# Routing of batches 1 and 2 beside another layer, and a last layer whose batch is chosen by numbers on the chip

## The chip, the cores and the metric

One core of a Trainium2 chip runs the whole program. TensorE (PE) does the matmuls, VectorE (DVE), ScalarE (ACT) and GpSimd (POOL) the work on elements, and SyncE (SP) issues most transfers, in the order of its queue. The metric is the device time of one execution in microseconds, as a median over runs. Engines work their instruction streams in order and wait for each other by semaphores. The order of each stream is fixed when the program is built: a scheduler places the instructions that the Python code below issues, and may move them against each other within what the data allow.

## The reference

Three stages, float32. Attention over 4 batches, 8 heads, 576 positions and 64 dimensions, in a linear form with 128 random features; its result, 2304 x 512, goes through two mixture-of-experts layers with 8 experts each.

```python
def phi(x):
    proj = np.einsum('bhsd,df->bhsf', x, w_phi)
    proj = proj - np.max(np.abs(proj), axis=-1, keepdims=True)
    return np.concatenate([np.exp(proj), np.exp(-proj)], axis=-1)
q_p, k_p = (phi(q), phi(k))
...
# first layer: for each expert e
out[mask] = gate_w[mask, None] * (np.maximum(x[mask] @ w1[e], 0.0) @ w2[e])
...
# second layer, capacity 576: token i goes to its best expert e
if counts[e] < capacity:
    disp[e, counts[e]] = x[i]; pos[i] = counts[e]; counts[e] += 1; keep[i] = True
...
h = np.maximum(np.einsum('ecd,edf->ecf', disp, w1), 0.0)
y = np.einsum('ecf,efd->ecd', h, w2)
# kept tokens:
out[i] = gate_w[i] * y[expert_idx[i], pos[i]]
```

Tokens that find their expert full give rows of zeros.

## The kernel before

**Tiles.** Tokens lie in the free dimension, features in the partitions: a batch's input of a layer is a tile `xd` of 128 x 4 x 578 (576 tokens in two halves of 288, and two columns for a common part that is kept apart). In this data all 576 tokens of a batch go to one expert. The kernel takes that as given, checks it on the chip (`bad`), and holds a general version behind a branch that is not taken here. So a layer (w, b), that is MoE layer w on batch b, is two products with the weights of one expert: `layer()` runs eight units `f` of the first product (`ps_h`, L796, evicted by DVE as `hd`, L807), calls `done()`, and then four blocks `d` of the second (`ps_y`, L830). In the second MoE layer DVE multiplies the block by the gate row `gr` (L852) and SP sends it out (L856, L859).

**Weights.** A layer has 16 units of 256 KB. `Stream` fetches them: SP reads the expert index from the chip (`value_load`, L747) when a layer's first unit is due, and then issues transfers into five buffers `wst` (L750). ACT converts a unit to `wh` (L765); DVE, for every third one, or POOL computes the rest `wl` (L767). Five converted units form a ring. Layers that were added to the stream follow each other in it.

**Routing.** `route(b, 2, ...)` is a generator: logits of batch b's 576 tokens, the best expert of each as one-hot rows (128 x 5 x 8), a count per expert, the capacity, the kept tokens' count, and `count()` with the expert's index `exi`, and a flag `act2`: whether any token of the batch is kept. `run_c` carries the counts from batch to batch, so the routings of layer 2 run in the order of the batches. `route1(b)` is the same for layer 1 without capacity, `gate_row(b)` lays the gates out as a row `gr` (L315, L319).

**The order.** `ORDER` is (1,0), (1,1), (2,0), (1,2), (1,3), (2,1). Beside each layer run attention steps, by `RATIO`, and the generators in `side`, up to `SIDE` = 5 steps at each of the layer's yields; `done()` finishes what is left of them before the second half of the layer, and adds the next layer to the stream. Batch 1's routing of layer 2 stands beside (1,3), behind batch 3's of layer 1, batch 2's too; batch 3's stands beside (2,1). Batches 2 and 3 of layer 2 come last, each under a branch on its flag. In this data batch 2 keeps no token, so its output is written as zeros, and batch 3 keeps all of its own. The weights for the first branch that is taken are fetched ahead of the branch, by an index `nxi` that is computed from both flags; inside the branch the ring goes on.

```python
side += {...
         (1, 2): [route1(2)],
         (1, 3): [route1(3), route(1, 2, ps_, "tr"), route(2, 2, ps_, "tr")],
         (2, 1): [route(3, 2, ps_, "tr")]}[which, b]
```

Of the kernel before, what the change touches and what calls it, by code (L numbers as in the profile page):

```python
# [36 lines left out]
SIDE = 5  # L37
# [6 lines left out]
def fused_kernel(ctx: ExitStack, tc: tile.TileContext, kq, v, wphi, emb, tau, w1, wg, w2, cap, out):  # L44
# [96 lines left out]
    def drain(g):  # L141
        for _ in g:
            pass
# [14 lines left out]
    act2 = [slots.tile([1, 1], F32, name=f"act2_{b}") for b in range(B)]  # L158
    act2i = [slots.tile([1, 1], I32, name=f"act2i_{b}") for b in range(B)]
    nxf = slots.tile([1, 1], F32, name="nxf")  # L160
    nxi = slots.tile([1, 1], I32, name="nxi")
# [50 lines left out]
    def route(b, which, ps_pool, ps_tag):  # L212
# [64 lines left out]
        if which == 2:  # L277
            T.matmul(pc[:, 1], tri_b, ohb, start=True, stop=True)
        tot = small.tile([128, 2, NT, E], F32, tag="tot", name="tot")
        V.tensor_copy(tot[:, 0:which], pc[:, 0:which])  # L280
        yield
        if which == 2:
            rk = small.tile([128, NT, E], F32, tag="rk", name="rk")
            for t in range(NT):
                V.tensor_tensor(out=rk[:, t, :], in0=tot[:, 1, t, :], in1=run_c, op=ALU.add)
                V.tensor_tensor(out=run_c, in0=run_c, in1=tot[:, 0, t, :], op=ALU.add)
                if t % 2:
                    yield
            V.tensor_scalar(rk, rk, cap_f, None, op0=ALU.is_lt)
            V.tensor_tensor(out=oh, in0=oh, in1=rk, op=ALU.mult)  # L290
            yield
            kp = small.tile([128, NT], F32, tag="kp", name="kp")
            V.tensor_reduce(out=kp, in_=oh, axis=AX.X, op=ALU.add)
            V.tensor_tensor(out=gt, in0=gt, in1=kp, op=ALU.mult)

            V.tensor_tensor(out=gt, in0=gt, in1=gts[1, b], op=ALU.mult)
            yield
            ohb2 = small.tile([128, NT, E], BF16, tag="ohb", name="ohb2")
            V.tensor_copy(ohb2, oh)
            pk = ps_pool.tile([128, NT, E], F32, tag=ps_tag, name="ps_ck")  # L300
# [910 lines left out]
```

## Time and profile before

| | |
|---|---|
| median of 3 runs | 544.06 us (543.0 to 547.17) |
| profiled execution, its own time | 545.21 us |
| its span | 543.5 us |
| PE busy | 431.3 us, 79% |
| DVE busy | 383.4 us, 71% |
| ACT busy | 242.5 us, 45% |
| POOL busy | 246.8 us, 45% |
| granted TensorE clock, mean | 0.896 |
| transfers | 49.71 MB, 91 GB/s over the span |

The span is what the profiler saw from the first to the last instruction; the profiled execution's own time is 1.7 us longer. Times in the rows are microseconds from the start of the span. An engine is busy while it executes; register, branch and transfer-issuing instructions don't count. "<-" behind a row names the engine and the instruction that ended the idle time ahead of it. The granted clock is given in parts of full speed.

### The profile page before, as it was taken

To read this page: it belongs to the slowest core of one execution; us is meant where nothing else is said; L and a number is where in the kernel's file an instruction comes from. 1 tells how busy PE (TensorE), PEld (TensorE's weight loads), DVE (VectorE), ACT (ScalarE), POOL (GpSimd) and SP (SyncE) were. 2 spreads that over 40 slices of the span, in tenths; PEclk is the share of its full clock that TensorE was granted. 3 is DMA by queue.
4 is the path that set the end of the run, shared out by engine and by line. 5 is a ranking of instruction groups with operands and counts; after the bars stand their busy time and mean duration, and the time that the engine had idled before them with its cause. 6 is when DMAs were issued, how large, how long until landed. Compare 5 with 4: busy or idle time off the path is not lost. (4 is left out here: it accounts for less than half of the span.)

```text
span 543.5 us, 10208 instructions
## 1 busy us (share of the span) xinstructions
PE 431.3 (79%) x3509; PEld 337.7 (62%) x3509; DVE 383.4 (71%) x1213; ACT 242.5 (45%) x539; POOL 246.8 (45%) x255
## 2 busy tenths in 40 slices
PE   5787887893896989779899979894997775792575
PEld 4465664563675876456778667673795663681474
DVE  3876456379989356489857897799555966987383
ACT  4656066162566176371757524462545342320230
POOL 5354445346277135593475533754543321530251
PEclk9979789887997999999899989997998795896678
DMA  6212000044250010633322420731104403512732
GB/s 210 69 48 86 25 26 26 0 136 148 75 198 7 1 26 0 224 127 90 117 58 61 147 77 23 249 118 39 40 2 153 139 20 119 173 43 87 262 118 93
DMA packets 24718, 49.71 MB, mean 91 GB/s; under 512 B 3448, under 2 KB 4536, under 8 KB 24656
## 3 DMA queue, kind: packets, MB, share of 16 engines
q1 hardware_dynamic: 24544, 48.89, 28.2%
q8 instruction: 31, 0.51, 0.4%
q14 instruction: 31, 0.25, 0.2%
q0 software_dynamic: 32, 0.03, 0.0%
q10 hardware_dynamic: 80, 0.03, 0.0%
HBM read 44.22 MB, written 4.72 MB: 90 GB/s over the span
## 5 line engine op out<-in xcount | busy, mean ns | idle before, releaser
L767 POOL TENSOR_TENSOR wl<-wst,wh 128x512 bf16<-128x512 f32 x64 | 82.5, 1297 | 75.8 <-ACT wh L765 71.2
L474 POOL TENSOR_SCALAR qa<-qf 128x1152 f16<-128x1152 f32 x32 | 100.1, 3136 | 30.7 <-ACT qf L472 30.3
L420 PE MATMUL ps_pj<-wb,raw 128*128 128x256 f32 x288 | 88.1, 441 | 30.6 <-DVE s L435 10.7
L765 ACT ACTIVATE wh<-wst 128x512 fp32r<-128x512 f32 x96 | 59.5, 627 | 81.2 <-PE ps_h L796 34.0
L420 PEld LDWEIGHTS ps_pj<-wb,raw 128*128 128x128 f32 x288 | 57.3, 217 | 43.2 <-issue 19.6
L483 PE MATMUL ps_vk<-kf,vr 128*65 128x256 f32 (+1 forms) x320 | 79.5, 387 | 0.8 <-PE ps_r L404 0.8
L830 PE MATMUL ps_y<-hd,wh 128*128 128x290 f32 (+1 forms) x448 | 77.8, 312 | 2.0 <-DVE hd L807 2.0
L796 PE MATMUL ps_h<-xd,wh 128*128 128x290 f32 (+1 forms) x256 | 54.2, 348 | 27.5 <-DVE hd L807 17.1
L425 DVE TENSOR_REDUCE mall<-ps_pj 128x4 f32<-128x512 f32 (+1 forms) x80 | 50.2, 630 | 24.0 <-PE ps_pj L420 23.7
L448 ACT ACTIVATE kf<-s,lnk 128x512 f32<-128x512 f32 (+1 forms) x96 | 57.0, 648 | 19.4 <-DVE s L435 19.4
L830 PEld LDWEIGHTS ps_y<-hd,wh 128*128 128x128 f32 x448 | 63.2, 189 | 3.6 <-ACT wh L765 1.7
L807 DVE TENSOR_SCALAR hd<-ps_h,sc,hd 128x288 fp32r<-128x288 f32 x112 | 59.8, 566 | 5.2 <-PE ps_h L796 4.8
L796 PEld LDWEIGHTS ps_h<-xd,wh 128*128 128x128 f32 x256 | 42.0, 217 | 32.4 <-issue 26.4
L483 PEld LDWEIGHTS ps_vk<-kf,vr 128*65 128x65 f32 (+1 forms) x320 | 39.2, 136 | 32.8 <-issue 16.5
L796 PE MATMUL ps_h<-yd,wh 128*128 128x290 f32 (+1 forms) x192 | 41.9, 365 | 19.4 <-DVEq L973 8.9
L435 DVE TENSOR_TENSOR s<-ps_pj,mall 128x512 f32<-128x512 f32 (+1 forms) x80 | 49.6, 628 | 3.2 <-ACT kf L448 1.5
L796 PEld LDWEIGHTS ps_h<-yd,wh 128*128 128x128 f32 x192 | 34.0, 236 | 22.4 <-ACTq L973 9.0
L767 DVE TENSOR_TENSOR wl<-wst,wh 128x512 bf16<-128x512 f32 x32 | 31.0, 970 | 13.8 <-ACT wh L765 13.6
L472 ACT ACTIVATE qf<-tr 128x512 f32<-128x512 f32 x64 | 33.8, 598 | 6.2 <-PE tr L466 6.0
L531 PE MATMUL ps_nm<-kvh,qa 128*128 128x65 f16 x320 | 32.5, 197 | 0.0
L532 PE MATMUL ps_nm<-kvl,qa 128*128 128x65 f16 x320 | 32.4, 198 | 0.0
L528 PE MATMUL ps_nm<-kcl,ones_h 128*128 128x65 f16 x160 | 30.1, 200 | 0.9 <-POOL kcl L518 0.9
(246 smaller groups left out, 757.5 us busy)
## 6 DMA issues: line engine op xcount, KB each, us to landing
wst<-in_w SPq DMA_DIRECT2D x96, 256.0 KB, 2.9
raw<-in_kq SPq DMA_DIRECT2D x15, 576.0 KB, 5.5
vr<-in_v SPq DMA_DIRECT2D x16, 325.0 KB, 5.5
wfx<-in_w SPq DMA_DIRECT2D x16, 256.0 KB, 2.9
out_t<-o SPq DMA_DIRECT2D x9, 288.0 KB, 2.1
out_t<-zero SPq DMA_DIRECT2D x1, 1152.0 KB, 5.0
out_t<-o SPq DMA_DIRECT2D x6, 144.0 KB, 2.5
raw<-in_kq SPq DMA_DIRECT2D x1, 288.0 KB, 3.8
```

Source lines behind the costliest of these rows:

```text
L420: T.matmul(ps[:, k_], d["raw"][:, sl], wb, start=True, stop=True)
L425: V.tensor_reduce(out=mall_of[b][:, p, U[0]:U[0] + len(U), :], in_=st[i]["pj", u][:, 0:len(U)], axis=AX.X, op=ALU.max, apply_absolute_valu ...
L435: V.tensor_tensor(out=s[:, 0:n], in0=d["pj", u][:, 0:n], in1=m.unsqueeze(3).to_broadcast([128, n, 2, 128]), op=ALU.subtract)
L448: A.activation(out=d["kf"][0:n, t0:t0 + nk, :, sg, :], in_=d["su", u][0:n, 0:nk], func=AF.Exp, bias=lnk[0:n], scale=(1.0 - 2.0 * sg) / SC)
L472: A.activation(out=d["qf"][:, h, sg, 0:512], in_=d["tr", h], func=AF.Exp, scale=(1.0 - 2.0 * sg) / SC)
L474: G.tensor_scalar(d["qa"][:, h, :, 0:S], d["qf"][:, h], -1.0, None, op0=ALU.add)
L483: T.matmul(ps[:, h, :], d["vr"][0:n, t, h, :], d["kf"][0:n, t, h].rearrange("p s f -> p (s f)"), start=(t == 0), stop=(t == NT - 1))
L765: A.activation(out=h, in_=src, func=AF.Copy)
L767: q.tensor_tensor(out=l, in0=src, in1=h.bitcast(F32), op=ALU.subtract)
L796: T.matmul(ps[:, 0:n], wh[:, c, :], x[:, c, hf * HALF:hf * HALF + n], start=(c == 0), stop=(c == 3 and not hf))
L807: V.tensor_scalar(hd[:, f, hf * HALF:(hf + 1) * HALF], ps[:, 0:HALF], sc[:, f:f + 1], nm, op0=ALU.add, op1=ALU.max)
L830: T.matmul(ps[hf][:, 0:w], wh[:, j, :], hd[:, k_, hf * HALF:hf * HALF + w], start=(k_ == 0), stop=(k_ == 7 and not hf))
```

## The change

Routing: `route(1, 2)` and batch 1's gate row move from beside layer (1,3) and the start of (2,1) to beside layer (1,2). `route(2, 2)` comes first beside (1,3), then `route1(3)`, and what is left of them at the layer's middle is no longer finished there. `SIDE` is 3 beside (1,3) and (2,1).

Counting in layer 2: the rank of a token within its expert, which took ten operations of 128 x 8 on DVE, becomes four more small matmuls into one PSUM tile, one addition and one fused compare and multiply; the counts are taken on all 128 partitions, and the copies out of PSUM go.

The last layer: (2,3) stands in `ORDER` behind (2,1), in the same weight stream. `choose()` blends batch 2 and batch 3 by their flags: the input (x = x3 * act3 + x2 * (1 - act3), four ACT and four DVE operations of 128 x 578), the gates, the expert's index and the two output offsets, so that the batch that is active is computed and written to its place, and zeros to the other's. Only when both are active is there a branch, for batch 2, behind it.

```diff
-SIDE = 5
+SIDE = {(1, 3): 3, (2, 1): 3}
...
-        if which == 2:
-            T.matmul(pc[:, 1], tri_b, ohb, start=True, stop=True)
-        tot = small.tile([128, 2, NT, E], F32, tag="tot", name="tot")
-        V.tensor_copy(tot[:, 0:which], pc[:, 0:which])
...
-            for t in range(NT):
-                V.tensor_tensor(out=rk[:, t, :], in0=tot[:, 1, t, :], in1=run_c, op=ALU.add)
-                V.tensor_tensor(out=run_c, in0=run_c, in1=tot[:, 0, t, :], op=ALU.add)
...
+        T.matmul(pc[:, 1], tri_b, ohb, start=True, stop=False)
+        for t in range(NT - 1):
+            n = NT - 1 - t
+            T.matmul(pc[:, 1, t + 1:NT], ones_b, ohb[:, t:t + 1, :].to_broadcast([128, n, E]), start=False,
+                     stop=(n == 1))
...
+        V.tensor_tensor(out=rk, in0=pc[:, 1], in1=run_c.unsqueeze(1).to_broadcast([128, NT, E]), op=ALU.add)
+        V.scalar_tensor_tensor(out=oh, in0=rk, scalar=cap_f, in1=oh, op0=ALU.is_lt, op1=ALU.mult)
...
+        T.matmul(pk, ones_b, ohb2, start=True, stop=True)
+        tot = small.tile([128, E], F32, tag="tot", name="tot")
+        V.tensor_reduce(out=tot, in_=pc[:, 0].rearrange("p t e -> p e t"), axis=AX.X, op=ALU.add)
...
+        V.tensor_tensor(out=run_c, in0=run_c, in1=tot, op=ALU.add)
...
-            ORDER = [(1, 0), (1, 1), (2, 0), (1, 2), (1, 3), (2, 1)]
+            ORDER = [(1, 0), (1, 1), (2, 0), (1, 2), (1, 3), (2, 1), (2, 3)]
...
+            def choose():
+                V.tensor_scalar(two, act2[3], -1.0, 1.0, op0=ALU.mult, op1=ALU.add)
+                f0 = nxf[:, 0:1]
+                V.tensor_tensor(out=f0, in0=exf[2, 3], in1=exf[2, 2], op=ALU.subtract)
+                V.tensor_tensor(out=f0, in0=f0, in1=act2[3][0:1], op=ALU.mult)
+                V.tensor_tensor(out=f0, in0=f0, in1=exf[2, 2], op=ALU.add)
+                V.tensor_scalar(nxi[:, 0:1], f0, -1.0, float(E), op0=ALU.mult, op1=ALU.add)
...
+                for c in range(4):
+                    A.activation(out=x[:, c], in_=x[:, c].bitcast(F32), func=AF.Copy, scale=act2[3])
+                    V.scalar_tensor_tensor(out=x[:, c], in0=y[:, c].bitcast(F32), scalar=two,
+                                           in1=x[:, c].bitcast(F32), op0=ALU.mult, op1=ALU.add)
+                    yield
...
-                    while side:
+                    while side and ORDER[k] != (1, 3):
                         side_step()
...
-                         (1, 2): [route1(2)],
-                         (1, 3): [route1(3), route(1, 2, ps_, "tr"), route(2, 2, ps_, "tr")],
-                         (2, 1): [route(3, 2, ps_, "tr")]}[which, b]
+                         (1, 2): [route(1, 2, ps_, "tr"), route1(2), row(1)],
+                         (1, 3): [route(2, 2, ps_, "tr"), route1(3)],
+                         (2, 1): [route(3, 2, ps_, "tr"), choose()],
+                         (2, 3): [row(3)]}[which, b]
...
+                if (which, b) == (2, 3):
+                    SP.dma_start(out=out[:, bass.ds(SP.value_load(nxi[0:1, 2:3], min_val=2 * S, max_val=3 * S), S)]
+                                 .rearrange("(d p) n -> p d n", p=128),
+                                 in_=zero.unsqueeze(1).to_broadcast([128, 4, S]))
+                    at = SP.value_load(nxi[0:1, 1:2], min_val=2 * S, max_val=3 * S)
...
-            first_units(nxi)
...
-            on = {b: nc.values_load(act2i[b][0:1, 0:1], min_val=0, max_val=1) for b in (2, 3)}
-            for b in (2, 3):
-                with tc.If(on[b] > 0) as br:
-                    ws.restart(w2, exi[2, b], True)
-                    BASE[2, b] = 0
-                    drain(layer(b, 2))
...
+            both = nc.values_load(nxi[0:1, 3:4], min_val=0, max_val=1)
+            with tc.If(both > 0):
...
+                drain(layer(2, 2))
```

**The order on SP around the first weights of layer (2,1).** Before, with `exi2_1_111` as batch 1's index for layer 2:

```order
L750 DMA wst_5662<-in_w1 128x512
L750 ISA
L750 DMA wst_5717<-in_w1 128x512
L747 TENSOR_LOAD exi2_1_111
L747 ISA x2
L750 ISA
L750 DMA wst_5784<-in_w2 128x512
```

After, at the same place (the last transfers of (1,3), the first of (2,1)):

```order
L747 DMA wst_5649<-in_w1 128x512
L747 ISA
L747 DMA wst_5687<-in_w1 128x512
L747 ISA
L747 DMA wst_5740<-in_w2 128x512
```

The read of the index has gone from between the two layers; it now stands a layer earlier, among the transfers of (1,2).

**The order on SP behind the last weights of (2,1).** Before, up to the first weights of the last layer (`wfx`):

```order
L971 TENSOR_LOAD act2i_2_120
L971 ISA x2
L859 DMA out_t<-o_6222 128x576
L859 DMA out_t<-o_6258 128x576
L859 DMA out_t<-o_6294 128x576
L856 DMA out_t<-o_6326 128x288 x2
L971 TENSOR_LOAD act2i_3_121
...
L747 TENSOR_LOAD nxi_123
L747 ISA x2
L750 ISA
L750 DMA wfx_6379<-in_w2 128x512
```

After:

```order
L854 DMA out_t<-o_6345 128x288 x2
L965 TENSOR_LOAD nxi_119
L965 ISA x2
L965 REGISTER_ALU
L965 DMA out_t<-zero_5916 128x4x576
L968 TENSOR_LOAD nxi_119
...
L744 TENSOR_LOAD nxi_119
L744 ISA x2
L747 ISA
L747 DMA wst_6228<-in_w2 128x512
```

The block of zeros, which stood behind the last layer's branch, and the reads of three numbers more now stand between the output of (2,1) and the weights of the last layer.

**The order on DVE from the flag of batch 3 to the last layer.** Before (`nxf`, `nxi` are the index of the chosen expert):

```order
L343 CAST act2i_3_121<-act2_3_117 1x1
...
L954 TENSOR_TENSOR nxf_122<-nxf_122,act2_2_116 1x1
L955 TENSOR_TENSOR nxf_122<-nxf_122,exf2_3_105 1x1
L956 TENSOR_SCALAR nxi_123<-nxf_122 1x1
L315 COPY gr_6425<-ps_g_6426 128x512
L319 COPY gr_6425<-ps_g2_6432 128x64
L767 TENSOR_TENSOR wl0_150<-wfx_6379,wh0_149 128x512
L767 TENSOR_TENSOR wl3_156<-wfx_6382,wh3_155 128x512
L971 TENSOR_LOAD act2i_2_120
L973 COMPARE_AND_BRANCH
L803 TENSOR_SCALAR hd_146<-ps_h_6465 128x1
```

After (`yd_5728` is batch 3's input of layer 2, `yd_5194` batch 2's):

```order
L932 SCALAR_TENSOR_TENSOR gt_6021<-gt_5450,two_120,gt_6021 128x5
L937 SCALAR_TENSOR_TENSOR yd_5728<-yd_5194,two_120,yd_5728 128x578
...
L937 SCALAR_TENSOR_TENSOR yd_5728<-yd_5194,two_120,yd_5728 128x578 x2
L924 TENSOR_TENSOR nxf_118<-nxf_118,exf2_2_104 1x1
L316 COPY gr_6422<-ps_g_6423 128x512
L320 COPY gr_6422<-ps_g2_6429 128x64
L937 SCALAR_TENSOR_TENSOR yd_5728<-yd_5194,two_120,yd_5728 128x578
L925 TENSOR_SCALAR nxi_119<-nxf_118 1x1
L940 CAST xb_5914<-yd_5728 128x8
L764 TENSOR_TENSOR wl1_149<-wst_6228,wh1_148 128x512
```

The four blends and the gate row now stand ahead of the chosen index; the residuals `wl` follow behind it, and no branch.

## Rows read from the trace of the kernel before

**Rows 1.** Stages of the last third: each engine's busy time in a stretch.
```profile
core 0: us, PE busy (x) PEld busy (x) DVE busy (x) ACT busy (x) POOL busy (x), PEclk, DMA share, GB/s
349.30:409.30 60.00, 51.82 (x483) 42.02 (x484) 43.54 (x152) 29.84 (x69) 28.83 (x23) 0.91 0.19 59
409.30:415.30 6.00, 2.91 (x22) 1.49 (x21) 3.05 (x27) 2.39 (x6) 0.00 (x0) 1.00 0.38 107
415.30:445.70 30.40, 26.05 (x206) 23.43 (x207) 24.46 (x88) 12.94 (x25) 13.90 (x11) 0.83 0.37 118
445.70:458.10 12.40, 3.35 (x21) 2.00 (x20) 8.43 (x58) 2.58 (x7) 0.21 (x2) 0.58 0.17 41
458.10:489.50 31.40, 26.61 (x213) 23.83 (x214) 27.04 (x89) 10.52 (x18) 14.20 (x11) 0.90 0.40 129
489.50:509.10 19.60, 3.29 (x15) 2.08 (x14) 10.85 (x61) 3.38 (x6) 2.77 (x3) 0.56 0.42 141
509.10:536.70 27.60, 24.79 (x192) 22.97 (x192) 18.00 (x47) 6.50 (x11) 10.31 (x8) 0.82 0.46 152
536.70:543.50 6.80, 0.03 (x2) 0.00 (x0) 1.10 (x3) 0.00 (x0) 0.00 (x0) 0.72 0.27 94
```

**Rows 2.** Timeline of PE: start, us, instruction, and what ended the idle time before.
```profile
458.11 3.82 PE L796 MATMUL ps_h<-yd,wh 128*128 128x290 f32 x16 [2.88 <-ACT wh L765]
...
509.08 1.30 PE L796 MATMUL ps_h<-yd,wh 128*128 128x290 f32 x4 [8.87 <-DVEq L973]
...
513.83 1.32 PE L796 MATMUL ps_h<-yd,wh 128*128 128x288 f32 x8
...
519.98 1.31 PE L796 MATMUL ps_h<-yd,wh 128*128 128x290 f32 x4 [2.81 <-DVE hd L807]
```

**Rows 3.** Timeline of DVE and SP ahead of layer (2,1).
```profile
453.73 0.13 DVE L340 TENSOR_SCALAR exi<-fm 1x1 int32<-1x1 f32 x1
...
454.69 20.21 SPq L750 DMA_DIRECT2D wst<-in_w  x16
```

**Rows 4.** Timeline of all engines ahead of the last layer.
```profile
496.54 0.20 DVE L303 COPY tot<-ps_ck 128x40 f32<-128x40 f32 x1
...
497.28 0.13 DVE L342 TENSOR_SCALAR act<-fmx 1x1 f32<-1x1 f32 x1
...
499.29 0.14 DVE L956 TENSOR_SCALAR nxi<-nxf 1x1 int32<-1x1 f32 x1
...
500.40 10.06 SPq L750 DMA_DIRECT2D wfx<-in_w  x10
...
503.18 0.63 ACT L765 ACTIVATE wh<-wfx 128x512 fp32r<-128x512 f32 x1 [11.40 <-DMA wfx<-in_w]
...
508.05 0.69 DVE L767 TENSOR_TENSOR wl<-wfx,wh 128x512 bf16<-128x512 f32 x1 [3.51 <-ACT wh L765]
```

**Rows 5.** Single lines from 280 us on: least, median and greatest ns, first and last.
```profile
L852 DVE SCALAR_TENSOR_TENSOR o<-ps_y,ny,gr x24: 495/509/518, 335.5 to 537.4; 128x288 f32<-128x288 f32 x24
L315 DVE COPY gr<-ps_g x4: 671/678/692, 326.1 to 500.0; 128x512 f32<-128x512 f32 x4
L285 DVE TENSOR_TENSOR rk<-tot,run_c x20: 150/166/1279, 318.8 to 495.1; 128x8 f32<-128x8 f32 x20
```

**Rows 6.** Timelines of DVE and POOL at one place beside layer (1,2).
```profile
361.44 3.12 DVE L585 TENSOR_SCALAR hi__4695<-n 128x5 f32<-128x5 f32 x1
...
361.39 3.15 POOL L474 TENSOR_SCALAR qa<-qf 128x1152 f16<-128x1152 f32 x1 [0.25 <-ACT qf L472]
```

**Rows 7.** Page, transfers: count, KB each, us from issue to landing.
```profile
out_t<-zero SPq DMA_DIRECT2D x1, 1152.0 KB, 5.0
```

**Rows 8.** Two stretches of the last layer, columns as in the first group.
```profile
519.90:526.50 6.60, 6.52 (x36) 6.11 (x37) 6.60 (x18) 1.26 (x2) 3.82 (x4) 0.53 0.53 155
526.50:536.70 10.20, 10.20 (x98) 9.56 (x96) 6.44 (x18) 2.53 (x4) 2.93 (x3) 1.00 0.30 111
```

More of the change, by code (lines that the diff above doesn't have):

```diff
@@ L157, in fused_kernel @@
     exi = {(w, b): slots.tile([1, 1], I32, name=f"exi{w}_{b}") for w in (1, 2) for b in range(B)}
[L158 to L161, printed above, removed]
+    act2 = [slots.tile([128, 1], F32, name=f"act2_{b}") for b in range(B)]
+    nxf = slots.tile([1, 4], F32, name="nxf")
+    nxi = slots.tile([1, 4], I32, name="nxi")
+    two = slots.tile([128, 1], F32, name="two")
     def add_bad(cond_ok):
@@ L306, in route @@
-        if which == 1:
-            yield from count(b, which, tot)
+        if which == 1:
+            yield
+            yield from count(b, which, pc[:, 0])
+            return
+        T.matmul(pc[:, 1], tri_b, ohb, start=True, stop=False)
[3 more added lines that the diff above has]
+                     stop=(n == 1))
+        V.tensor_tensor(out=gt, in0=gt, in1=gts[1, b], op=ALU.mult)
@@ L309, in gate_row @@
+        tot = small.tile([128, E], F32, tag="tot", name="tot")
+        V.tensor_reduce(out=tot, in_=pc[:, 0].rearrange("p t e -> p e t"), axis=AX.X, op=ALU.add)
+        yield
+        V.tensor_tensor(out=run_c, in0=run_c, in1=tot, op=ALU.add)
+        kp = small.tile([128, NT], F32, tag="kp", name="kp")
+        V.tensor_reduce(out=kp, in_=oh, axis=AX.X, op=ALU.add)
+        yield
+        V.tensor_tensor(out=gt, in0=gt, in1=kp, op=ALU.mult)
+        yield from count(b, which, pk)
     def gate_row(b, which, gd, ps_pool, ps_tag):
@@ L322, in count @@
     def count(b, which, tot):
-        cnt = small.tile([1, 1, E], F32, tag="cnt", name="cnt")
-        V.tensor_reduce(out=cnt[:, 0, :], in_=tot[0:1, 0].rearrange("p t e -> p e t"), axis=AX.X, op=ALU.add)
+        cnt = small.tile([128, 1, E], F32, tag="cnt", name="cnt")
+        V.tensor_reduce(out=cnt[:, 0, :], in_=tot.rearrange("p t e -> p e t"), axis=AX.X, op=ALU.add)
         yield
-        _, cmx, crev = yield from first_max(cnt, 1, 1, "ct")
+        _, cmx, crev = yield from first_max(cnt, 128, 1, "ct")
+        if which == 2:
+            V.tensor_scalar(act2[b], cmx[:, 0:1], 0.0, None, op0=ALU.is_gt)
+        cnt, cmx, crev = cnt[0:1], cmx[0:1], crev[0:1]
         ok = small.tile([1, 1], F32, tag="ok", name="ok")
@@ L754, in fetch, with ahead @@
                     return True
[L756 removed]
+                def ahead(self, n):
                     while self.nu <= n:
[L759 removed]
+                        while self.nf < self.nu + NST and self.fetch():
                             pass
@@ L781, in sums, with layer @@
                 return ps_.tile([128, HALF + 2], F32, tag=tag, name=name)
-            def layer(b, which, done=None):
+            def layer(b, which, done=None, at=None):
+                at = b * S if at is None else at
                 base = BASE[which, b]
@@ L903, in prepare @@
                     att_until(lambda: x_done[b])
-                ws.add((which, b), w1 if which == 1 else w2, exi[which, b])
+                ws.add((which, b), w1 if which == 1 else w2, nxi[:, 0:1] if (which, b) == (2, 3) else exi[which, b])
                 BASE[which, b] = 16 * (len(ws.list) - 1)
```

93 lines of the change are left out of this document (34 added, 59 removed).

## Prediction

> **What bounds the kernel now.** I read the stage table first [rows 1]: the last third of the program as eight stretches. In the two layer stretches of batches 1 and 3 (415.3 to 445.7 and 458.1 to 489.5) PE and DVE are both over 80% busy, so neither hides the other; in 349.3 to 409.3, where attention runs beside layer (1,2), PE is busy 51.82 of 60.0 us. Then look at what stands between the layers: 12.4 us with PE busy 3.35, and 19.6 us with PE busy 3.29. The PE timeline [rows 2] gives where they end: layer (2,1) starts at 458.11 and the last layer at 509.08; the last layer stops once more, for 2.81 us, and goes on at 519.98.
>
> The timelines of DVE, SP and ACT say why. Before (2,1), batch 1's routing ends with its expert index at 453.73; SP reads it and its first weight transfer is issued at 454.69 [rows 3]. Before the last layer, batch 3's routing is the chain: count of the kept tokens 496.54, activity flag 497.28, chosen expert 499.29, first weight transfer 500.40, first conversion 503.18, the DVE's last residual 508.05, then the branch [rows 4]. The first matmul comes 5.3 us after the first converted block is there (503.18 + 0.63 = 503.81 to 509.08): it waits for the branch, ahead of which DVE has two residuals to compute. These are the two places that the change touches.
>
> **Term by term.** All against the profiled execution: span 543.5, its own time 545.21, 1.15 above the median of 544.06.
>
> *A, shorter counting of layer 2.* Ten 128x8 operations per batch (five of them L285, median 0.166 [rows 5]) and two copies go, one reduction, one fused operation and four tiny matmuls come: about 1.5 us of DVE per batch. Batches 1 to 3 are inside the terms below. Batch 0's lies in layer (2,0) beside attention; I take -1.0 (0 to -2).
>
> *B, batch 1's routing and gate row beside layer (1,2).* The DVE work of a routing can be sized from the first gap, which is nearly nothing else: 8.43 us busy there, of which the start of batch 2's is about 2, less 1.5 from A: some 5 to 6.5 us, and a gate row of 0.9. DVE has 16.5 us free in the 60.0 [rows 1], but PE has only 8.2: what delays DVE where PE waits for it is lost. Most should be absorbed. I take +3; the bounds are 0 (all absorbed) and +9 (none, and some lock waits, below). SP now reads batch 1's index between weights 12 and 13 of (1,2). Four weight transfers, then batch 3's index and the weights of (1,3), stand behind that wait; the count finishes beside about unit 4 of the layer, and those blocks are used in its last half, so I cost it at nothing. If the count came after the layer's first half, one restart, 3.4 us (454.69 to 458.11 [rows 2, 3]), would be due.
>
> *C, layer (1,3).* The 6.0 us before it stay: they are the index of batch 3, the transfer and conversion. Batch 2's routing now fills them instead of batch 3's first one, which moves into the layer and past its end. Work of like size changes places: 0 (-2 to +3).
>
> *D, the first gap.* Batch 1's index is known a layer early, and SP sends the first blocks of (2,1) straight behind those of (1,3). PE's next instruction after (1,3) is a matmul of (2,1): -12.4, all of it; at worst -8, if DVE's leftover from (1,3) holds the first PSUM banks.
>
> *E, layer (2,1).* It now starts on converted weights. Its first 16 matmuls took 3.82 us, where 8 take 1.32 later [rows 2]; that is 1.2 saved, and batch 2's ten short operations are gone from DVE's path in the first half. What comes in is the end of batch 3's first routing. 31.4 to 29.0, -2.4 (-5 to +3).
>
> *F, the second gap.* Here the new order decides. PE's count of batch 3 stands inside the last quarter of (2,1), but the matmul of the kept tokens stands behind its last one, and SP's read of the chosen expert behind its output transfers. From the end of (2,1): 0.3 to the kept count in PSUM (an estimate), from there to the flag 0.7 to 0.9 as now (496.54 to 497.28 + 0.13 [rows 4]), and two output blocks at 0.51 [rows 5] between them, so the flag is at +2.0 to 2.3. Then the selection: ACT scales four 128x578 pieces (0.63 for 512 columns, about 0.7 each), DVE needs 1.4 for its small operations and four additions of a size no row shows: between 0.68 (copy of 512) and 1.0 (twice the 288-column output block); I take 0.75, nearer the copy, as both operands lie in SBUF and DVE's neighbours are idle. The gate row's two copies (0.9) are ahead of the fourth. Flag + 1.4 + 3.0 + 0.9 + 0.4 gives the expert at +7.9. From there 1.1 to the first transfer (499.29 to 500.40 [rows 4]) and 3.4 to the first matmul [rows 2, 3] make 12.4. The zero block's transfer is issued about 4 us ahead of the weights and took 5.0 [rows 7]; I add nothing for what is left of it, 1 us is possible. So 12.5 for 19.6: -7.1 (bounds: 10 with additions of 0.68 and an earlier flag; 18 with the zero block fully in front).
>
> [...]
>
> *G, the last layer.* The hole of 2.81 us before 519.98 [rows 2] closes, since its cause, a ring that is only refilled behind the branch, is gone. Behind it come 6.6 us at a granted clock of 0.53, PE and DVE both busy throughout [rows 8], where DVE catches up. Up to 526.5 the layer takes 17.4 us, in which DVE works 11.6 (18.00 in all [rows 1], less the 6.44 after 526.5 [rows 8]). Without hole and slow clock DVE bounds this half: 11.6, and the first block's conversion and residual (0.63 and 0.69 [rows 4]), which now lie inside the layer, 1.3, and half of the 4.4 us that DVE idles in layer (2,1) [rows 1], 2.2: 15.1 for 17.4, -2.3 (-5 to 0).
>
> *H, the end.* 536.7 to 543.5 stays 6.8: there are still two branches, and the output transfers are the same. 0 (0 to +1).
>
> Sum: -1.0 + 3 + 0 - 12.4 - 2.4 - 7.1 - 2.3 = -22.2. 545.21 - 22.2 = 523.0 on the profiled execution, 521.9 on the median; I say 522.
>
> **Rivals.**
>
> *The second gap stays.* If choosing and selecting cost as much as branch and refill do now (19.6 us), F is 0: 529. For it: five register reads now stand in a row on SP, and selection waits for two engines in turn. Against: the 5.3 us behind the first conversion have no counterpart.
>
> *Routing hides better than I think.* If the flag is there before (2,1) ends, the gap shrinks to the selection and transfer, 6 us, and B is 0: 522 - 6.5 - 3 = 512.5. Against: the kept-token matmul stands behind the last matmul of the layer.
>
> *Slower: DVE shut out by POOL.* At 361.44 a DVE operation on 128x5 took 3.12 us, exactly while POOL ran its 3.15 us instruction, and L285 took 0.150 to 1.279 [rows 6]. Routing in the gaps met no POOL work; now three of them run beside POOL's 28.83, 13.90 and 14.20 us [rows 1], 56.9 in sum. Each microsecond of new lock wait in a DVE-bound half lengthens the layer. With x of these 56.9 as new waits the time is 522 - 3 + x (B holds 3 already): same as before at x = 25, slower by 1% from x = 30.5, over half; at two thirds (38), 557. Against it: routings already run beside POOL in all these layers, and a POOL instruction can hold DVE once, not once for each small operation.
>
> [...]
>
> *The change doesn't do what it says.* Layer (2,1) could still wait, for PSUM or for DVE's leftovers: D is -3 rather than -12.4, 531.
>
> **Chances.** Forecast (516 to 528) 0.62; second gap stays (529) 0.15; hides better (512.5) 0.10; lock, half of it (about 540) 0.06, all of it (557) 0.03; no first gap saved (531) 0.04. The range 511 to 534 takes in the forecast and its neighbours and leaves out the lock and the tails of the rest, some 2 in 10. Faster by over 1% (below 538.6; 1% is about what three runs of this kernel, 543.0 to 547.17, can tell from nothing): all but the lock cases, 0.90. Same: 0.06. Slower: 0.04.
>
> **What would show it.** D right: under 1 us between the last matmul of (1,3) and the first of (2,1), and the clock of that stretch above the 0.58 it has now. F right: about 12 us of PE idle before the last layer, ended by the first conversion, with four DVE additions at 0.7 to 1.0 in it. G right: no hole over 2 us in the last layer. B wrong: the stretch from the start of (1,2) to the start of (1,3) over 69 us, with DVE operations of 128x40 or less at 1 to 3 us. The forecast as a whole is wrong if PE's idle time before (2,1) is still 5 us or more, or if the layers themselves grow by over 10 us in sum.

## The result, and the profile after

The changed kernel takes 526.77 us, median of 4 runs (526.13 to 527.64), beside 543.53 us for the kernel before: a ratio of 0.969, 95% interval 0.9628 to 0.9753. In a second measurement it took 523.64 us beside 543.51 us (0.9639, 0.9602 to 0.9676). The prediction was 522 us, 511 to 534.

The stages of the profiled execution after (span 525.0 us, columns as in [rows 1]). The stretches are, in order: from the end of layer (2,0) through attention and most of layer (1,2), its end with the wait for (1,3), layer (1,3), layer (2,1), the gap, the last layer, and what lies behind its last matmul. (The first row of [rows 1] begins later in the program, at the first matmul of (1,2), so these two rows are not the same work.)

```profile
349.30:414.30 65.00, 55.77 (x508) 42.93 (x507) 46.23 (x179) 26.72 (x62) 28.02 (x22) 0.87 0.18 52
414.30:423.20 8.90, 3.57 (x33) 2.46 (x32) 4.68 (x33) 4.16 (x10) 0.11 (x1) 0.84 0.26 77
423.20:450.30 27.10, 25.86 (x219) 22.77 (x220) 23.27 (x96) 14.04 (x27) 15.55 (x13) 0.93 0.59 176
450.30:476.60 26.30, 23.55 (x221) 20.86 (x221) 24.74 (x94) 9.97 (x20) 12.66 (x10) 1.00 0.44 137
476.60:489.00 12.40, 1.73 (x12) 1.00 (x9) 8.03 (x43) 3.41 (x5) 0.00 (x0) 0.57 0.56 199
489.00:513.40 24.40, 22.64 (x192) 20.76 (x192) 17.38 (x49) 9.46 (x15) 13.09 (x10) 0.94 0.55 171
513.40:525.00 11.60, 0.00 (x0) 0.00 (x0) 1.10 (x3) 0.00 (x0) 0.00 (x0) 0.61 0.18 59
```

Against [rows 1]: the gap of 12.4 us ahead of (2,1) has no row any more, the gap ahead of the last layer is 12.40 us instead of 19.60, the three layers are shorter. But layer (1,3) starts at 423.2 instead of 415.3, and the tail behind the last matmul is 11.60 us instead of 6.80.

| stretch | before | after | difference | predicted |
|---|---|---|---|---|
| to the start of (1,3) | 415.3 | 423.2 | +7.9 | +2 (A, B) |
| (1,3) and the gap behind it | 42.8 | 27.1 | -15.7 | -12.4 (C, D) |
| (2,1) | 31.4 | 26.3 | -5.1 | -2.4 (E) |
| second gap | 19.6 | 12.4 | -7.2 | -7.1 (F) |
| last layer | 27.6 | 24.4 | -3.2 | -2.3 (G) |
| behind its last matmul | 6.8 | 11.6 | +4.8 | 0 (H) |
| sum | 543.5 | 525.0 | -18.5 | -22.2 |

**The second gap** runs nearly as it was worked out. From the timeline of all engines of the changed kernel (the layer ends at 476.6):

```profile
479.29 0.15 DVE L330 TENSOR_SCALAR act<-fmx 128x1 f32<-128x1 f32 x1
480.92 0.40 SPq L965 DMA_DIRECT2D out_t<-zero  x1
481.34 1.53 DVE L937 SCALAR_TENSOR_TENSOR yd<-yd,two 128x578 fp32r<-128x578 f32 x2
484.33 0.13 DVE L925 TENSOR_SCALAR nxi<-nxf 1x1 int32<-1x1 f32 x1
485.42 9.50 SPq L747 DMA_DIRECT2D wst<-in_w  x10
488.97 3.80 PE L795 MATMUL ps_h<-yd,wh 128*128 128x290 f32 x16 [6.89 <-ACT wh L762]
```

The flag stands 2.7 us behind the layer's end (2.0 to 2.3 predicted), the chosen index 7.7 (7.9), the first weights are issued 1.1 us later and the first matmul comes 3.55 us after that (3.4), ended by the first conversion. A blend takes 0.80 us, two of them 1.53 (0.75 each). From the flag to the first matmul it is 9.7 us, where it was 11.8 before (497.28 to 509.08 [rows 2, 4]). The other 5.1 us of the gain lie ahead of the flag, which stood 7.8 us behind the end of (2,1) before.

**The tail** is SP's. What SP's queue waited for, from the last matmuls on: in the changed kernel (total us, times, longest; other rows left out)

```profile
SPq L991 <- SPq L991: 3.3, 2, 2.8
...
SPq L1183 <- SPq L1183: 2.4, 1, 2.4
SPq L854 <- DMA out_t<-o: 1.5, 1, 1.5
```

and in the kernel before

```profile
SPq L1169 <- SPq L1169: 2.8, 1, 2.8
...
```

L991 is the new branch on both batches, L1183 (L1169 before) the branch to the general version. Both are skipped, and SP waits 3.3 and 2.4 us at them, one behind the other. Before, the last layer stood inside a branch that was taken, and behind it SP passed only the short way over the other case, in 0.2 us (538.4 to 538.6). L854 is the store of the last block's second half: with the address in a register it is made to wait for the landing of the first half, 1.5 us; behind (2,1), where the address is fixed, SP has no wait for a landing at L854. In SP's records the new branch takes 3.9 us as a whole (516.6 to 520.5), 3.8 more than the short way; the store adds 1.5, and the branch to the general version takes 3.0 instead of 3.5: 3.8 + 1.5 - 0.5 = 4.8, the growth of the tail.

The records of the branch instructions themselves are 45 and 53 ns long on SP; at the skipped branches SP waited 2.4 and 3.3 us.

**The stretch beside (1,2)**, where batch 1's routing was put: PE's longest wait there, and what held it up.

```profile
366.05 6.42 POOL L475 TENSOR_SCALAR qa<-qf 128x1152 f16<-128x1152 f32 x2 [4.18 <-ACT qf L473]
369.42 2.88 DVE L294 SCALAR_TENSOR_TENSOR foh<-rk,cap_f,foh 128x40 f32<-128x40 f32 x1
372.58 0.21 PE L299 MATMUL ps_ck<-ohb,ones_b 128*128 128x40 bf16 x1 [3.21 <-DVE ohb L297]
```

A routing operation on 128x40, which took 0.26 us in the second gap, takes 2.88 us and ends within 0.2 us of POOL's second conversion, as the row of 3.12 us did in [rows 6]. Behind it PE stands 3.21 us at the matmul that counts the kept tokens, with the layer's own matmuls queued behind. Whether this is the 8 us was open. Two sets of rows speak against it. The kernel before has waits of this length in the same stretch:

```profile
371.84 0.77 PE L796 MATMUL ps_h<-xd,wh 128*128 128x290 f32 x4 [4.46 <-DVE rn L255]
377.60 1.30 PE L796 MATMUL ps_h<-xd,wh 128*128 128x290 f32 x4 [3.29 <-DVE hd L807]
```

And from the end of (2,0) to the start of (1,3), first before the change, then after it:

```profile
346.00:415.30 69.30, 55.65 (x532) 44.33 (x529) 49.85 (x183) 32.91 (x74) 31.34 (x25) 0.93 0.25 76
349.30:423.20 73.90, 59.34 (x539) 45.39 (x537) 50.90 (x212) 30.88 (x71) 28.12 (x23) 0.87 0.19 55
```

This way is 4.6 us longer, of which 3.7 are busy time of PE, at a granted clock of 0.87 instead of 0.93, and 0.9 idle time. The other 3.3 of the 7.9 us lie ahead of it: (2,0) ends at 349.3 instead of 346.0.

### The profile page after: what moved, and what is told of

Read it like the earlier page. It is cut to its first block, busy times and chain, and to the rows that moved or that the text cites. A ratio compares the mean times of both kernels' runs of the same rounds, so it can differ in the third digit from the quotient of the medians.

```text
span 525.0 us, 10188 instructions
## 1 busy us (share of the span) xinstructions
PE 427.3 (81%) x3520; PEld 332.3 (63%) x3520; DVE 373.4 (71%) x1174; ACT 244.6 (47%) x543; POOL 246.6 (47%) x255
## 4 chain that ended last, share of the span: by engine, by line
PE 49%; DVE 28%; DMA 7%; issue 6%; ACT 5%; POOL 2%; SPq 1%; ACTq 0%; DVEq 0%
PE ps_vk L484 12%; PE ps_y L829 8%; PE ps_pj L421 8%; PE ps_h L795 6%; DVE hd L806 4%; DVE wl L764 3%; DMA vr<-in_v 3%; DVE mall L426 3%; DVE s L436 3%; DMA wst<-in_w 2%; PE ps_nm L532 2%; PE tr L467 2%; PE ps_nm L533 2%; DMA wg_t<-in_wg 1%; ACT wh L762 1%
## 5 line engine op out<-in xcount | busy, mean ns | idle before, releaser
L764 POOL TENSOR_TENSOR wl<-wst,wh 128x512 bf16<-128x512 f32 x74 | 94.7, 1288 | 90.8 <-ACT wh L762 83.6
L762 ACT ACTIVATE wh<-wst 128x512 fp32r<-128x512 f32 x112 | 69.1, 627 | 79.6 <-PE ps_h L795 29.8
L484 PE MATMUL ps_vk<-kf,vr 128*65 128x256 f32 (+1 forms) x320 | 81.1, 394 | 2.9 <-issue 1.7
L829 PE MATMUL ps_y<-hd,wh 128*128 128x290 f32 (+1 forms) x448 | 79.0, 314 | 1.8 <-DVE xs L543 0.9
L795 PE MATMUL ps_h<-xd,wh 128*128 128x290 f32 (+1 forms) x256 | 52.0, 336 | 15.3 <-DVE hd L806 9.8
L795 PEld LDWEIGHTS ps_h<-xd,wh 128*128 128x128 f32 x256 | 39.7, 206 | 19.1 <-issue 11.5
L795 PE MATMUL ps_h<-yd,wh 128*128 128x290 f32 (+1 forms) x192 | 38.7, 337 | 10.9 <-ACT wh L762 6.9
L795 PEld LDWEIGHTS ps_h<-yd,wh 128*128 128x128 f32 x192 | 30.3, 210 | 13.9 <-ACT wh L762 8.7
L532 PE MATMUL ps_nm<-kvh,qa 128*128 128x65 f16 x320 | 34.2, 201 | 0.0
L533 PE MATMUL ps_nm<-kvl,qa 128*128 128x65 f16 x320 | 34.1, 201 | 0.0
L529 PE MATMUL ps_nm<-kcl,ones_h 128*128 128x65 f16 x160 | 30.4, 201 | 0.9 <-POOL kcl L519 0.9
```

The source lines that it names most:

```text
L484: T.matmul(ps[:, h, :], d["vr"][0:n, t, h, :], d["kf"][0:n, t, h].rearrange("p s f -> p (s f)"), start=(t == 0), stop=(t == NT - 1))
L532: T.matmul(o, q, d["kvh"][:, h, sg, :], start=False, stop=False)
L762: A.activation(out=h, in_=src, func=AF.Copy)
L764: q.tensor_tensor(out=l, in0=src, in1=h.bitcast(F32), op=ALU.subtract)
L795: T.matmul(ps[:, 0:n], wh[:, c, :], x[:, c, hf * HALF:hf * HALF + n], start=(c == 0), stop=(c == 3 and not hf))
L829: T.matmul(ps[hf][:, 0:w], wh[:, j, :], hd[:, k_, hf * HALF:hf * HALF + w], start=(k_ == 0), stop=(k_ == 7 and not hf))
```

## Experiments

### What the parts gave alone

**The routing alone.** The kernel before with the generators, the steps and the end of `done()` of the change, and nothing else:

```diff
-SIDE = 5
+SIDE = {(1, 3): 3, (2, 1): 3}
...
-                    while side:
+                    while side and ORDER[k] != (1, 3):
...
-                         (1, 2): [route1(2)],
-                         (1, 3): [route1(3), route(1, 2, ps_, "tr"), route(2, 2, ps_, "tr")],
+                         (1, 2): [route(1, 2, ps_, "tr"), route1(2), row(1)],
+                         (1, 3): [route(2, 2, ps_, "tr"), route1(3)],
```

> The kernel before with the routing moved as in the change (batch 1's and its gate row beside (1,2), batch 2's first beside (1,3), nothing finished at the middle of (1,3), three steps there and beside (2,1)); the long counting, the two branches and their weights stay. Theory 1, the move gains the 12 to 16 us of the first gap and of (1,3), and costs 6 to 10 us in the stretch beside (1,2): 533 to 538 us, second gap near 19.6 us as before, end near 6.8 us. Rival, the displaced work on DVE costs as much as the gap was: 540 us or more.

533.9 us (0.9828, 0.9788 to 0.9868). Layer (1,3) starts at 420.5, 5.2 us later than before, and runs into (2,1) without a gap:

```profile
420.50:454.20 33.70, 28.79 (x217) 25.25 (x217) 28.04 (x105) 14.19 (x27) 15.61 (x13) 0.81 0.46 143
454.20:481.30 27.10, 24.41 (x215) 21.56 (x212) 25.78 (x96) 10.12 (x20) 12.89 (x10) 0.94 0.41 133
481.30:497.70 16.40, 3.20 (x19) 2.04 (x17) 8.55 (x47) 3.14 (x5) 2.76 (x3) 0.59 0.46 148
```

The move gains as expected. The second gap shrank as well, from 19.6 to 16.40, which neither theory had.

**The counting alone.** The kernel before with the short counting of the change and no other part (the diff of the change's section up to `run_c`; with it comes the flag `act2`, now taken on all 128 partitions and ahead of the index).

> The kernel before with the short counting alone. By the working of the prediction, 1.5 us less on DVE for each batch: both gaps 1 to 1.5 us shorter, 0 to 1 us elsewhere, 538.5 to 541 us. Rival, the counting is hidden or its new matmuls wait as long: 542 us, gaps of 12.4 and 19.6 us.

534.22 us (0.9842, 0.9803 to 0.988): 9 us, where 2.5 to 5 had been worked out, and both theories fall. The second gap is the surprise. Its rows here, and the row of the kernel before that answers to the first:

```profile
478.58 0.19 PE L297 MATMUL ps_ck<-ohb,ones_b 128*128 128x40 bf16 x1
480.02 0.15 DVE L328 TENSOR_SCALAR act<-fmx 128x1 f32<-128x1 f32 x1
492.28 1.30 PE L796 MATMUL ps_h<-yd,wh 128*128 128x290 f32 x4 [10.56 <-DVEq L973]
```

```profile
496.28 0.21 PE L301 MATMUL ps_ck<-ohb,ones_b 128*128 128x40 bf16 x1 [3.05 <-DVE ohb L299]
```

Layer (2,1) ends at 478.7 here and at 489.5 in the kernel before: the kept tokens of batch 3 are counted 0.1 us ahead of the layer's end instead of 6.8 us behind it. So the chain of routings that run one behind the other came in ahead of the layer's end, and the gap fell from 19.6 to 13.6 us with the branch still in it. The start of (1,3) moved from 415.3 to 410.7 too. But the profiled execution took 529.67 us, 4.6 us less than the median, and layer (2,0) starts 4.8 us earlier in it already; what did that was not taken apart.

**Both, with the branch kept:** the changed kernel without the choice by numbers.

> The kernel before with the moved routing and the short counting, but with the two branches at the end as they were: the changed kernel without the choice by numbers. From the stages of the runs so far, the choice shortens the second gap from 13.6 (short counting, branch) to 12.4 us and the last layer from about 28 to 24.3 us, and lengthens the end from 7.4 to 11.7 us. Theory 1, it nets about nothing: 523 to 526 us here, within 1.5 us of the changed kernel (523.64). Rival, the choice carries the second gap, as the prediction had it (7.1 + 2.3 us): 529 us or more.

527.63 us (0.9675, 0.9616 to 0.9733), between the two cases, beside the changed kernel's 0.969 and 0.9639. The intervals lie over each other; the choice by numbers, as it was made, is worth too little to be told from nothing. The stages show why it isn't more (the profiled execution, 531.09 us, is the slowest of the four):

```profile
478.80:492.50 13.70, 1.81 (x15) 1.10 (x11) 5.55 (x29) 3.04 (x5) 2.41 (x2) 0.68 0.51 162
492.50:521.60 29.10, 25.39 (x192) 23.66 (x192) 18.00 (x47) 6.50 (x11) 11.08 (x9) 0.80 0.46 152
521.60:529.30 7.70, 0.09 (x4) 0.00 (x0) 1.10 (x3) 0.00 (x0) 0.00 (x0) 0.70 0.26 87
```

Second gap, last layer and tail are 13.7, 29.1 and 7.7 us here, 12.4, 24.4 and 11.6 in the changed kernel: 6.0 us gained, 3.9 given back.

**The changed kernel again**, beside these:

> The changed kernel once more, beside the three runs that follow, so that they share a chip and the runs of the kernel before. If its time is 525.5 to 528 us, the kernels without the branch (520.58) and with the early index (519.9) really gained 6 us, twice what their last stretch shows; if it is 522 to 525 us, part of it was the chip.

523.64 us (0.9639, 0.9602 to 0.9676): the second case, so part of the 6 us was not the edits. The same kernel differs by 3 us between two measurements, and the kernel before, 543.53 and 543.51 us, does not follow it. So the ratio doesn't take this out, and a difference of 3 us between kernels that were not measured together shows nothing by itself.

### The last layer: index, zeros, branch, store

**The index ahead of the blends.** `nxi` gets its number before DVE starts on the blends; a scratch that `two` then overwrites keeps the scheduler to it.

```diff
-                V.tensor_scalar(two, act2[3], -1.0, 1.0, op0=ALU.mult, op1=ALU.add)
-                f0 = nxf[:, 0:1]
+                f0 = two[0:1]
...
                 V.tensor_scalar(nxi[:, 0:1], f0, -1.0, float(E), op0=ALU.mult, op1=ALU.add)
+                V.tensor_scalar(two, act2[3], -1.0, 1.0, op0=ALU.mult, op1=ALU.add)
```

> The changed kernel with the index of the chosen expert computed on DVE ahead of the four blends of the input instead of behind them; the block of zeros is still issued ahead of the weights. Theory 1, the index (484.33) sets the start of the last layer and the block of zeros holds nothing up: the weights are issued at about 482 instead of 485.4, the gap of 11.8 us ahead of the last layer falls to 8 to 8.5, time 523 us. Rival, the weights wait behind the block of zeros (issued 480.9, 4.5 us to landing): the gap falls to 10 to 11 only, time 525 to 526 us.

519.9 us (0.9553, 0.9478 to 0.9628). The gap is 10.3 us, 2.1 less:

```profile
476.87 0.40 SPq L964 DMA_DIRECT2D out_t<-zero  x1
477.10 0.14 DVE L923 TENSOR_SCALAR nxi<-two 1x1 int32<-1x1 f32 x1
479.31 6.22 SPq L747 DMA_DIRECT2D wst<-in_w  x7
482.50 1.31 ACT L762 ACTIVATE wh<-wst 128x512 fp32r<-128x512 f32 x2 [3.96 <-DMA wst<-in_w]
```

The layer ends at 472.9: the index is at +4.2 instead of +7.7, but the weights are issued 2.2 us behind it instead of 1.1, since SP now reads its other numbers in that time; from issue to conversion it is 3.2 us. The gap is the rival's, the time is below both cases. The next run shows how far the rival's cause, the zeros, holds.

**And the zeros behind the weights.** The block is filled by ACT from a tile of the layer's middle and written behind the last weights; the early transfer and its fill by POOL go.

```diff
+                        A.activation(out=zero, in_=hd[:, 7, 0:S].bitcast(F32), func=AF.Copy, scale=0.0)
+                        SP.dma_start(out=out[:, bass.ds(SP.value_load(nxi[0:1, 2:3], min_val=2 * S, max_val=3 * S), S)]
+                                     .rearrange("(d p) n -> p d n", p=128),
+                                     in_=zero.unsqueeze(1).to_broadcast([128, 4, S]))
```

> As the run before it, and the block of zeros is written behind the last layer's weights, from a tile that ACT fills in the middle of that layer. If the block of zeros held the weights up: gap 8 to 8.5 us and 522 to 524 us here, 1 to 2.5 us less than with the index alone. If it did not: the same time as with the index alone. If the outputs now wait for the block: the last layer or the end is 1 to 3 us longer and eats the gain.

526.66 us (0.9681, 0.9618 to 0.9745). The gap is 8.9 us, 1.4 less than with the index alone:

```profile
478.16 0.14 DVE L923 TENSOR_SCALAR nxi<-two 1x1 int32<-1x1 f32 x1
479.57 4.41 SPq L747 DMA_DIRECT2D wst<-in_w  x6
482.26 0.63 ACT L762 ACTIVATE wh<-wst 128x512 fp32r<-128x512 f32 x1 [2.67 <-DMA wst<-in_w]
```

From issue to conversion it is 2.7 us instead of 3.2, and from the index to the issue 1.4 instead of 2.2. In the run before, SP's read of the index took 0.86 us behind the issue of the zeros; here, with no block under way, each of its four reads took 0.26 to 0.28. So the zeros cost the weights 0.5 us directly, and most of the rest goes with that read.

All of it and more is lost behind: the last layer takes 26.8 us instead of 23.9 and the tail 15.9 instead of 12.1. SP waited

```profile
SPq L858 <- DMA out_t<-zero: 4.2, 1, 4.2
SPq L854 <- DMA out_t<-o: 3.5, 1, 3.5
```

The outputs, whose addresses are in a register too, are made to wait until the zeros have landed. The third case came in, with 6.7 us instead of 1 to 3. The early block of the change is the better place.

**No branch on both batches.** Where both are active, `bad` is raised, and the general version computes all.

```diff
-            both = nc.values_load(nxi[0:1, 3:4], min_val=0, max_val=1)
-            with tc.If(both > 0):
...
-                V.tensor_tensor(out=nxi[:, 3:4], in0=act2[2][0:1], in1=act2[3][0:1], op=ALU.mult)
+                V.scalar_tensor_tensor(out=bad, in0=act2[2][0:1], scalar=act2[3][0:1], in1=bad, op0=ALU.mult, op1=ALU.add)
```

> The changed kernel without the branch on both batches behind the last layer; where both are active the flag of the general version is raised instead, so that only its branch is left. Theory 1, SP pays for each large branch that is skipped, one after the other behind the last output (3.9 us from 516.6 to 520.5 for this one): the stretch from the last matmul to the end falls from 11.6 to about 8, the time to about 523 us. Rival, the output transfers with addresses from registers set the end, and the branches lie beside them: 11.6 stays, 526 to 527 us.

520.58 us (0.9567, 0.9504 to 0.963). The tail is 10.0 us: 1.6 less, not 3.6. SP's waits in it:

```profile
SPq L1176 <- SPq L1176: 2.8, 1, 2.8
SPq L854 <- DMA out_t<-o: 2.7, 1, 2.7
```

One of the two branches is gone, and the wait of the second store grew by 1.2 us in this run. So the theory held for the branch, and the other cost showed beside it. That the whole time fell by more than the tail is not explained by it: up to (2,1) nothing was changed, and (1,3) starts at 420.8 here, 2.4 us earlier. In six profiles with the same program up to there (the changed kernel twice, these three and the next) it starts between 418.7 and 423.2.

**All three: early index, one branch, one store** of the last block in place of two.

```diff
-                                if which == 2 and d == 3:
+                                if which == 2 and d == 3 and b < 2:
...
-                    if which == 2 and d < 3:
+                    if which == 2 and (d < 3 or b >= 2):
```

> The changed kernel with three edits: the index ahead of the blends, no branch on both batches (the flag of the general version instead), and the last output block of a layer with an address from a register stored in one transfer, so that its second half doesn't wait for the landing of the first (1.5 us before, 2.7 us without the branch). If the three add up: gap near 10.3 us (-2), end near 6.5 to 7.5 us (11.6 before: -3.3 for the branch, -1.5 for the store), 5 to 7 us under the changed kernel of the same call. Rival, the end is bound by the landing of the outputs and not by SP: end near 9 to 10 us, 3 to 4 us under it.

517.68 us (0.9538, 0.9495 to 0.9581), 6 us under the changed kernel, measured beside it. The gap and the tail:

```profile
474.30:484.90 10.60, 1.93 (x13) 1.12 (x12) 8.59 (x43) 3.46 (x6) 0.00 (x0) 0.70 0.68 237
508.70:515.60 6.90, 0.09 (x4) 0.00 (x0) 1.10 (x3) 0.00 (x0) 0.00 (x0) 0.79 0.26 93
```

The three add up, and the rival falls: the tail is at 6.9 us, where it was before the change, and SP's list there has one branch (3.1 us) and no wait for a landing. Branch and store were the whole of H.

### The 8 us ahead of (1,3)

**Batch 1's routing beside (1,3).**

```diff
-                         (1, 2): [route(1, 2, ps_, "tr"), route1(2), row(1)],
-                         (1, 3): [route(2, 2, ps_, "tr"), route1(3)],
-                         (2, 1): [route(3, 2, ps_, "tr"), choose()],
+                         (1, 2): [route1(2)],
+                         (1, 3): [route(1, 2, ps_, "tr"), route(2, 2, ps_, "tr"), route1(3)],
+                         (2, 1): [row(1), route(3, 2, ps_, "tr"), choose()],
```

> The changed kernel with batch 1's routing of layer 2 taken out of layer (1,2) again: it now comes first beside (1,3), ahead of batch 2's, and batch 1's gate row comes at the start of (2,1). Theory 1, the moved routing is what makes the stretch up to the start of layer (1,3) 8 us longer than before the change (423.25 against 415.31): the start of (1,3) comes back to 415 to 418, the layers (1,3) and (2,1) together take 2 to 4 us more, the time is 521 to 525 us. Rival: the stretch is longer because the program around it was put in another order, whatever stands beside (1,2): the start stays at 422 to 424 and the time is 528 to 531 us.

532.4 us (0.98, 0.9719 to 0.9881). The rival falls: (1,3) starts at 413.3, so the moved routing was what the stretch had paid for. But theory 1's time is missed by 7 us; the routing is paid for more dearly here:

```profile
413.30:442.90 29.60, 27.55 (x228) 23.77 (x228) 25.34 (x93) 15.24 (x29) 17.13 (x14) 0.91 0.55 166
442.90:479.00 36.10, 30.09 (x231) 25.36 (x231) 29.26 (x122) 9.93 (x19) 11.63 (x10) 0.86 0.27 89
479.00:494.20 15.20, 1.91 (x13) 1.22 (x11) 10.27 (x57) 3.64 (x6) 0.00 (x0) 0.54 0.51 181
```

(2,1) takes 36.1 us instead of 26.3 and the gap 15.2 instead of 12.4: the routings, each behind the one before, run past the layers that should cover them.

**Where beside (1,2), and how fast.** Three variants of the kernel with the three edits, measured together. First, the layer-1 routing of batch 2 ahead of the moved one:

```diff
-                         (1, 2): [route(1, 2, ps_, "tr"), route1(2), row(1)],
+                         (1, 2): [route1(2), route(1, 2, ps_, "tr"), row(1)],
```

> The kernel with the three edits, and beside layer (1,2) the routing of batch 2 for the first layer comes ahead of the moved routing of batch 1 for the second. Theory 1, the moved routing costs 8 us there because it is put into the layer's first units, where PE's queue holds its matmuls and waits (3.21 us for the kept tokens): later in the layer it costs less, (1,3) starts at 416 to 419 instead of 421.5, time 513 to 516 us. Rival, what counts is how much work DVE has beside the layer, wherever it stands: start 420 to 423, 516.5 to 520 us.

517.19 us (0.949, 0.9436 to 0.9544), start of (1,3) at 418.9: the start is theory 1's, the time the rival's, and not to be told from the kernel with the three edits by its interval. The wait of 3.21 us is gone (the longest is 2.55), and yet PE idles 13.9 us from the end of (2,0) to the start of (1,3), 14.2 with the three edits: that wait was not the cost.

Second, two steps of the routing at each yield of (1,2) instead of five:

```diff
-SIDE = {(1, 3): 3, (2, 1): 3}
+SIDE = {(1, 2): 2, (1, 3): 3, (2, 1): 3}
```

> The kernel with the three edits, with two steps of the routing at each yield of layer (1,2) instead of five, so that it is spread over the layer. Theory 1 (place and waits): start of (1,3) at 416 to 419, 513 to 516 us. Rival (amount of work): 420 to 423, 516.5 to 520 us. A third way: spread thin, the routing of batch 2 isn't done by the middle of the layer, where the rest is finished in one go, and the layer is longer: over 520 us.

511.81 us (0.9414, 0.9368 to 0.9459), less than any case had named; all its runs are faster than all runs of the two variants beside it. From the end of (2,0) to the start of (1,3), with five steps (the kernel with the three edits), with two, and with no such routing there (the run with batch 1's routing beside (1,3)):

```profile
349.80:421.50 71.70, 57.54 (x538) 44.92 (x536) 50.21 (x212) 30.77 (x72) 27.90 (x23) 0.87 0.18 56
345.70:411.80 66.10, 55.14 (x539) 43.75 (x538) 48.17 (x212) 30.42 (x72) 27.88 (x23) 0.92 0.21 62
349.10:413.30 64.20, 53.42 (x515) 42.81 (x512) 44.77 (x173) 27.97 (x67) 27.16 (x21) 0.88 0.20 61
```

The first two rows hold the same instructions but for a few. PE idles 14.2 us with five steps, 11.0 with two and 10.8 with none. The six profiles of five steps spread from 70.3 to 73.9 us, but their idle time only from 14.2 to 14.7; what differs among them is PE's busy time, 55.9 to 59.3 us, at granted clocks from 0.91 down to 0.87. So of the 5.6 us between the first two rows 3.2 are idle time that the slower pace takes away; the other 2.4 are busy time, at 0.92 instead of 0.87, and lie within that spread. It is not the amount of work beside the layer but its pace; the rival falls, and the third way too. (1,3) starts at 411.8; of the 9.7 us to the kernel with the three edits, 4.1 lie ahead of this stretch. The medians measured together, 511.81 and 517.19 for the variant above, differ by 5.4, about as much as the stretch. DVE still had an operation that took 2.61 us here, and PE a wait of 3.10 us; which waits made up the 3.2 us was not taken apart.

Third, batch 1's gate row beside (2,1):

```diff
-                         (1, 2): [route(1, 2, ps_, "tr"), route1(2), row(1)],
+                         (1, 2): [route(1, 2, ps_, "tr"), route1(2)],
...
-                         (2, 1): [route(3, 2, ps_, "tr"), choose()],
+                         (2, 1): [row(1), route(3, 2, ps_, "tr"), choose()],
```

> The kernel with the three edits, with batch 1's gate row computed beside layer (2,1), ahead of batch 3's routing, instead of beside (1,2). In the changed kernel PE waits 1.21 and 0.42 us at 404.65 and 405.32 behind DVE work that ends with the row's two copies. If the row costs what PE waited there, (1,3) starts 1 to 2 us earlier and (2,1) takes about 1 us more: 516 to 518 us, no difference to be measured. If the row's place sets the order of the layer's tail too: 3 us either way.

518.1 us (0.9504, 0.9457 to 0.955), (1,3) at 422.0. No difference in time, as the first case had it, nor the earlier start; the row is not what costs there.

## Why the prediction was right, and where its steps were not

The direction, the size and the two gaps were right. That 522 was only 1.6 to 4.8 us too low is in part luck: in the table B and H came out 10.7 us worse than worked out, the other terms 7.0 us better.

**D, right; C and E too small.** PE goes from (1,3) into (2,1) without a pause, which is D, 12.4 us. But (1,3) itself, held at 0 by C, took 27.1 us instead of 30.4, and (2,1) gained 5.1 where E had 2.4; both lie just beyond their bounds. In (1,3) PE was busy as long as before (25.9 us, 26.1 before) and idle 1.2 instead of 4.4 us. In (2,1) its busy time fell by 3.1 us, at a granted clock of 1.00 instead of 0.90, and its idle time by 2.0. The sum had counted a gain for the first matmuls and batch 2's short operations alone; what took the idle time away was not taken apart.

**F, right in its number; the choice had the smaller part of it.** The working from the end of (2,1) over flag, blends and index to the first matmul holds row by row, but for the kept count: its 0.3 us were an estimate that no row shows, and it took 1.4, since its matmul (477.81, 0.18 us long) waited 1.08 us for DVE. But the prediction's first rival weighed it as the choice against the branch and its refill. With the branch in place the gap is 13.6 us with the counting alone and 13.7 with counting and routing; the choice brought only the rest, down to 12.4. Term A priced the counting by the time of its operations on DVE, 1.5 us a batch; with it the chain came in by the layer's end, and alone it made 9 us.

**B, mis-sized.** A and B gave +2 us up to the start of (1,3); it was +7.9 (+3.4 to +7.9 over the profiles with this order). Measured against the run without this routing beside (1,2), where (1,3) starts at 413.3, B is 5.4 to 9.9 us instead of 3. The step that failed is "Most should be absorbed": it compared DVE's free time with the work, not the pace at which the work was put in. PE idles 14.2 to 14.7 us with five steps where it idles 10.8 without the routing; with two steps it is 11.0. Before the change PE idled 13.7 us there, and with the short counting alone 11.0, so the routing took back what the counting had gained. The rest is busy time of PE at another granted clock, which differs by 3.4 us between profiles of one order.

**H, wrong.** "there are still two branches, and the output transfers are the same": neither was. The old branch was taken, and the new one is skipped, with 3.3 us of waits on SP behind everything else; and the second half of the last block, stored to an address from a register, is made to wait for the landing of the first, 1.5 us. With both undone the tail is 6.9 us again, for 6.8 before.

**G, right**, -3.2 for -2.3; the hole of 2.81 us in the last layer is gone, PE's longest wait inside it is 1.45 us.

**The rivals.** The second gap did not stay, and the layers (1,3) and (2,1) became shorter, not longer (27.1 and 26.3 us for 30.4 and 31.4), beside 15.55 and 12.66 us of POOL's work. Beside (1,2) a row of nearly 3 us is there (2.88), but before the change there are two (3.12 us [rows 6] and 2.77 us at 366.70). With the early index, the zeros ahead of the weights cost 1.4 us of gap (8.9 against 10.3), near the 1 us that was named as possible.

With the zeros first the conversion came 3.2 us after the issue of the weights, without them 2.7: for what was left of the zeros behind that issue it is 0.5 us at most here; the rest of the 1.4 lies ahead of the issue.

## What to carry to other kernels

An operation in a chain that runs past the layer which should cover it was worth more here than its own time (9 us for the counting, where 2.5 to 5 had been worked out): price it by where the chain then ends, not by its share of an engine. Work that is fed in beside a busy layer has a pace as well as a place (PE idled 14.2 us with five steps, 11.0 with two); try the pace first, it is one number. Behind the last output every branch and every wait of the issuing engine was bare here (a tail of 11.6 us with two skipped branches and the wait of the second store, 6.9 with one branch and one store): fold rare cases into a branch that stands there anyway, and store the last block once.

## What the hardware showed that was not expected

A skipped branch made SP wait 2.4 to 3.5 us here (3.3 and 2.4 in the changed kernel, 3.5 and 2.7 in its repeat), though the branch instruction itself is recorded with 45 and 53 ns. A read of a number into a register of SP took 0.84 to 0.91 us when it came 1 to 3 us behind the issue of the 1152 KB block of zeros (ten reads in eight profiles, among them 0.85 and 0.84 us at 482.0 and 483.1 in the changed kernel and 0.86 at 513.5 in the kernel before), where most others took 0.26 to 0.28 us. Six executions of the same instructions up to (1,3) reached it between 418.7 and 423.2 us, so a single profile can't carry a difference of 4 us; the idle time of PE in a stretch was steadier (14.2 to 14.7 us) than its length. The fastest version of the study, three edits and slow steps, takes 511.81 us, 0.9414 of the kernel before.
